# Retention plus switch MoE in one kernel: the order of rank, transpose and token steps around the first expert job, and the split of the last eviction

## The chip, the cores and the metric

The kernel runs on one core of a Trainium2 chip. The metric is the device time of one launch in microseconds (us), the median of several runs. All times below are microseconds unless marked ns; a time written like 98.18 is a moment, counted from the start of the profiled execution's span.

## What is computed

Inputs are q, k and v of shape (4, 8, 768, 64) in f32. The first stage is a retention (a linear attention whose state decays per head), the second a mixture of experts in which every token goes to one expert:

```python
gamma = 1.0 - 2.0 ** (-5.0 - np.arange(H))
for t in range(S):
    state = gamma * state + k[t] (outer) v[t]
    y[:, :, t] = q[t] @ state / sqrt(D)
x = y as (3072 tokens, 512)
logits = x @ w_gate + modality_bias[modality_id]
e = argmax(logits); gate = softmax(logits)[e]
out[token] = gate * (relu(x @ w1[e]) @ w2[e])      # w1: 512x1024, w2: 1024x512, 8 experts
```

## The kernel before

**Retention.** The 3072 tokens are 24 chunks of 128, six per batch entry. `two_chunks(n)` (L938) works on a pair of chunks at a time, and every engine gets its instructions in the order in which they are written there. For a pair n, n+1 the order on TensorE (PE) is: scores of the two chunks ahead (`scores`, L164, tile `sc`), the tokens of the two chunks behind (`tokens_out`, L216, tile `x`), the state part of the pair's heads (`heads_s`, L186, tile `y`), the masked part of chunk n (`heads_a`, L200, tile `y`), the state update of n+2 (`state`, L233, tile `st`), `heads_a(n+1)`, `state(n+3)`. VectorE (DVE) multiplies the scores by the mask into `abuf` (L176), scales the heads into `yT` (L214) and sums the gate logits `lg` (L229). ScalarE (ACT) scales q (`dq`, L153) and copies `x` out of PSUM into the token rows `xs` (L228) and the state `s` (L248). GpSimd (POOL) scales v (`vd`, L159).

**Buffers that tie the engines together.** All PSUM tiles come from one pool of eight banks, handed out in the order in which the readers of the earlier tiles are written; the state `st` holds one of them through a batch entry. The token rows `xs` have nine buffers (`XSB`, L44), so that the copy of chunk n waits until the rows of chunk n-9 have left.

**Routing.** After six chunks (a group; groups 0 to 3) the tokens get a place in the DRAM list `xsl`, ordered by expert: `route_a` (DVE; L315) makes the one-hot choice and the counts `cum`, `route_b` (PE, two small matmuls into `rk`; L353) the ranks, `route_c` (DVE; L360) the positions, `route_a` part 2 the gate's denominator (`den`, `rec`), and `scatter(g, i)` (POOL; L369) writes chunk i of the group to `xsl` with an indirect DMA (L378). Extra steps are hung into the pair loop with `at(n, place, ...)`, where the place is one of `top`, `st` (between the two scores), `sc` (after the second scores, or, in the pair's second half, between the two `heads_a`), `tk` (between the two `tokens_out`) and `end`.

**Jobs.** A job is 512 rows of one expert: 16 half stretches `first` (L714, tile `h_e` or `h_f`; six matmuls each, in three passes of split f32r numbers), then 16 `second` (L733, tile `o`). Weights are loaded with `raw` (L670, four buffers, issued on SyncE's queue), and split by `cut` (L675) into `hi` (ACT, L678) and `lo` (DVE, L683). The rows come with `rows_in` (L653, tile `xb`, SyncE's queue), are transposed by `flip_t` (DVE, L697) and split by `flip_hi` (ACT, L703) and `flip_lo` (DVE, L712). Two jobs (`e0`, `e1`) are chosen after group 1, at chunk 12, and the first starts when the last pair is done; group 3 is routed inside it: `last_tokens` (L1008) is a generator that goes on by one step after each stretch. Four further jobs (`f0` to `f3`) follow. The last job's last output tile is evicted from PSUM to `o` by DVE and ACT, half of the columns each (L750, L751), and then written by an indirect DMA (L754).

Of the kernel before, what the change touches and what calls it, by code (L numbers as in the profile page):

```python
# [11 lines left out]
AF = mybir.ActivationFunctionType  # L12
ALU = mybir.AluOpType
AX = mybir.AxisListType

P = 128
B, H, S, D = 4, 8, 768, 64
NT, DM, NE, DF = B * S, H * D, 8, 1024
NCH = S // P
NN = B * NCH  # L20
# [33 lines left out]
def kernel(  # L54
# [13 lines left out]
    nc = tc.nc  # L68
# [12 lines left out]
    def bank(name):  # L81
        return ps.tile([P, 512], F32, tag="bank", name=name)
# [133 lines left out]
    def tokens_out(n):  # L216
        yT, gr = yTs.pop(n), n // GRP
        if n % GRP == 0:
            lg[gr] = sm.tile([P, GRP, NE], F32, tag="lg", name=f"lg_{gr}")
        xs = xss[n] = wk.tile([P, NG, P + NE], F32, tag="xs", name=f"xs_{n}", bufs=XSB)  # L220
        for u in range(2):
            px = bank(f"x_{n}_{u}")[:, : 2 * (P + NE)].rearrange("p (g e) -> p g e", g=2)
            for g in range(2):
                nc.tensor.matmul(  # L224
                    px[:, g], yT[:, 2 * u + g], wgt[:, 2 * u + g], start=(g == 0), stop=(g == 1),
                    skip_group_check=True,
                )
            nc.scalar.copy(xs[:, 2 * u : 2 * u + 2], px)  # L228
        nc.vector.tensor_reduce(  # L229
            lg[gr][:, n % GRP], xs[:, :, P:].rearrange("p g e -> p e g"), axis=AX.X, op=ALU.add  # L230
        )
# [75 lines left out]
    def disjoint(ins, group):  # L307
        i = getattr(ins, "ins", ins)
        tc.declare_no_dep(i, group=group, reason="rows of different tokens")
        tc.add_to_no_dep_group(group, i)  # L310
# [42 lines left out]
    def route_b(gr):  # L353
        oh, ex = mid[gr]
        pr = bank(f"rk_{gr}")[:, : GRP * NE].rearrange("p (c e) -> p c e", e=NE)
        nc.tensor.matmul(pr, upper, oh, start=True, stop=False, skip_group_check=True)
        nc.tensor.matmul(pr, ones, cums[gr], start=False, stop=True, skip_group_check=True)
        mid[gr] = (oh, ex, pr)
# [59 lines left out]
    def ranks_a(t, counts):  # L418
        crep = sm.tile([P, NE, SPE], BF16, tag="crep", name=f"crep{t}")
        nc.vector.tensor_copy(crep, counts.unsqueeze(2).to_broadcast([P, NE, SPE]))  # L420
        mid["crep"] = crep.rearrange("p e i -> p (e i)")

    def ranks_p(t):
        crf = mid.pop("crep")
        pc = mid["pc"] = bank(f"pc{t}")
        nc.tensor.matmul(pc[:NCAND, :NCAND], ones[:, :NCAND], crf, start=True, stop=True)
        nc.tensor.matmul(pc[:NCAND, P : P + 1], crf, ones[:, 0:1], start=True, stop=True)
# [219 lines left out]
    def reg(lst, i, hi):  # L647
        return nc.values_load(lst[0:1, i : i + 1], engines=[SP], min_val=0, max_val=hi)

    def place(s, lst, i, j):  # L650
        s.row, s.e = reg(lst, i, EMPTY) * SLOT, reg(lst, j, NE - 1)
# [81 lines left out]
    def second(s, hh, part):  # L733
        if part == 0:
            s.po = bank(f"o{hh}_{s.tag}")
        for f in range(2 * part, 2 * part + 2):
            for k, (a, wi) in enumerate(PAIRS):
                nc.tensor.matmul(  # L738
                    s.po, s.hT[f][a][:, hh * P : (hh + 1) * P],
                    s.w[2][f // 2][wi][:, (f % 2) * DM : (f % 2 + 1) * DM],  # L740
                    start=(f == 0 and k == 0), stop=(f == FC - 1 and k == 2),
                )
        if part == 3:
            if hh == 0:
                s.o = me.tile([P, HH, DM], F32, tag="xb", name=f"o_{s.tag}")
            o = s.o[:, hh]
            gate = s.tg[:, hh, 1:2]
            if s is jobs[-1] and hh == HH - 1:
                h = DM // 2
                nc.vector.tensor_scalar(o[:, h:], s.po[:, h:], gate, None, op0=ALU.mult)  # L750
                nc.scalar.activation(o[:, :h], s.po[:, :h], AF.Copy, scale=gate)  # L751
            else:
                nc.scalar.activation(o, s.po, AF.Copy, scale=gate)  # L753
            ins = nc.gpsimd.indirect_dma_start(  # L754
                out=out[:, :],
                out_offset=bass.IndirectOffsetOnAxis(ap=s.tg.bitcast(I32)[:, hh, 0:1], axis=0),
                in_=o,
                in_offset=None,
                bounds_check=NT - 1,
                oob_is_err=False,  # L760
            )
            if s.tag != "dyn":
                disjoint(ins, "out_rows")
# [103 lines left out]
    def at(n, where, fn, *args):  # L867
        hooks.setdefault((n, where), []).append((fn, args))
# [12 lines left out]
    for g in range(NGRP - 1):  # L881
        t = (g + 1) * GRP
        at(t, "end", route_a, g, 0)
        at(t, "end", route_a, g, 1)
        at(t + 2, "st", route_b, g)
        early = g + 1 in EARLY
        if early:
            at(t + 2, "st", early_a, g + 1)
        at(t + 2, "st", route_c, g)
        at(t + 2, "st", route_a, g, 2)  # L890
        if early:
            a, b = EARLY[g + 1]
            at(t + 2, "st", early_b, g + 1)
            at(t + 2, "st", pick, a)
            at(t + 2, "end", place_early, a)
            at(t + 3, "end", mark, a)
            at(t + 3, "end", pick, b)
            at(t + 3, "end", mark, b)
            at(t + 3, "end", taken_a)
            at(t + 5, "end", taken_b)  # L900
            at(t + 4, "end", place_early, b)
        places = [(2, "end"), (3, "sc"), (4, "sc"), (4, "end"), (6, "sc"), (6, "end")]
        if early or t + 6 == NN:
            places[2:] = [(4, "sc"), (4, "end"), (5, "sc"), (5, "end")]
        for i, (k, where) in enumerate(places):
            at(t + k, where, scatter, g, i)

    t = GRP * min(EARLY)
    e = jobs[0]
    at(t + 2, "end", two, raw, e, 1, (0, 1))  # L910
    at(t + 3, "sc", two, raw, e, 1, (2, 3))
    at(t + 6, "top", rows_in, e)
    at(t + 6, "sc", cut, e, 1, 0, True)
    at(t + 6, "end", raw, e, 2, 0)
    n = t + 8
    at(n, "sc", flip_t, e, 0)
    at(n, "sc", flip_hi, e, 0)
    at(n, "tk", flip_lo, e, 0)
    at(n + 2, "top", flip_t, e, 1)
    at(n + 2, "top", flip_hi, e, 1)  # L920
    at(n + 2, "tk", flip_lo, e, 1)
# [85 lines left out]

    def last_tokens():  # L1008
        g = NGRP - 1
        tokens_out(NN - 1)  # L1010
        assert not hooks, hooks
        yield
        yield
        route_a(g, 0)
        yield
        yield
        route_a(g, 1)
        ranks_a("f", cnt[NGRP])
        yield
        yield  # L1020
        yield
        yield
        route_b(g)
        ranks_p("f")
        yield
        route_c(g)
        route_a(g, 2)
        yield
        scatter(g, 0)
        scatter(g, 1)  # L1030
        yield
        final_b()
        scatter(g, 2)
        scatter(g, 3)
        yield
        scatter(g, 4)
        scatter(g, 5)
        yield
        yield
        yield  # L1040
        final_c()
        yield
        final_d()
        for i in range(NLAST):
            place(jobs[NEARLY + i], lists["final"], i, U + i)
        for i, s in enumerate(rests):
            s.row = reg(lists["ends"], 1 + i, EMPTY) * SLOT
            s.e = reg(lists["final"], U + NLAST + i, NE - 1)
        yield
# [49 lines left out]
    with tc.manual_schedule(engines={PE, ACT, DVE, SP}):  # L1099
        load_kq(0, True)  # L1100
        nc.scalar.dma_start(cst, consts)
        nc.scalar.dma_start(gates, wgate)
        load_kv(0, True)
        load_kq(1)
        nc.sync.dma_start(dcq, decq)
        load_kv(1)
        for n in range(SINGLE, LEAD, 2):
            loads(n)
            if n == SINGLE + 2:
                setup_loads()  # L1110
        decay_v(0)
        at(0, "end", setup_a)
        at(1, "sc", setup_b)
        at(2, "sc", setup_rows)
        at(8, "end", setup_stores)
        at(5, "top", setup_c)
        at(7, "sc", list_consts)
        scores(0)
        for n in range(SINGLE):
            one_chunk(n)  # L1120
        first_pair(SINGLE)
        for n in range(SINGLE, NN, 2):
            two_chunks(n)
        tokens_out(NN - 2)
        r = last_tokens()
        for _ in all_jobs():
            next(r, None)
        assert next(r, "end") == "end"
# [4 lines left out]
    with tc.For_i(NLAST, nun, 1) as iv:  # L1133
        s = Job("dyn")
# [115 lines left out]
```

## Time and profile before

| | us |
|---|---|
| median of 3 runs | 391.22 |
| lowest and highest run | 389.74, 391.63 |
| the profiled execution | 389.86 |
| its span, first to last instruction | 388.0 |
| PE busy in the span | 371.4 |

The profile gives the busy time of each engine, a timeline (start, duration, engine, line, operation, output<-inputs, shapes, count of merged instructions, and in brackets the idle time of the engine just before, with what ended it), and tables of waits. PE means TensorE matmuls. Instructions of the same kind that follow each other on one engine are merged into one row, so a row's duration can hold gaps.

### The profile page before, as it was taken

The page shows a single profiled execution, that of the slowest core. Times are in us where ns is not written, and L with a number is a line of the kernel's source. Part 1 is how long each engine was busy: PE and PEld are TensorE (multiplying, and loading weights), DVE is VectorE, ACT ScalarE, POOL GpSimd, SP SyncE. Part 2 cuts the span into 40 slices and gives each one's busy share as a digit, 9 for nine tenths or more (in the row PEclk, how much of TensorE's full clock was granted, in tenths as well). Part 3 has the DMA queues.
Part 4 walks back from the last instruction along what each step waited for, and adds up shares of the span by engine and source line. Part 5 has one row for each costly group of instructions (what it writes and reads, how often), then busy time and mean ns, then how long its engine had stood idle before and what let it go on. Part 6 is the DMA issues. An engine that isn't in the chain of part 4 may idle for free.

```text
span 388.0 us, 7932 instructions
## 1 busy us (share of the span) xinstructions
PE 371.4 (96%) x2963; PEld 312.2 (80%) x2963; DVE 203.0 (52%) x417; ACT 156.6 (40%) x303; POOL 99.7 (26%) x141
## 2 busy tenths in 40 slices
PE   3999999999799999999999999999999999999993
PEld 3999898898688788888887888778888888888882
DVE  1676867778578982348343282433823466144100
ACT  1355536454566352435433354234532345234110
POOL 1342375574710787100220102101021002100121
PEclk9999999999999999999999999999999999999998
DMA  7999799999439758587972969729342584400001
GB/s 268 398 377 398 299 312 359 349 406 212 182 102 238 221 227 303 200 173 244 329 313 66 213 215 328 300 82 193 110 162 110 148 176 135 164 28 3 27 27 52
DMA packets 40330, 81.94 MB, mean 211 GB/s; under 512 B 8029, under 2 KB 20445, under 8 KB 40033
## 3 DMA queue, kind: packets, MB, share of 16 engines
q1 hardware_dynamic: 34720, 65.72, 53.8%
q0 software_dynamic: 5136, 15.21, 10.0%
q8 instruction: 25, 0.41, 0.5%
q10 hardware_dynamic: 432, 0.46, 0.4%
q14 instruction: 17, 0.14, 0.1%
HBM read 65.05 MB, written 23.41 MB: 228 GB/s over the span
## 4 chain that ended last, share of the span: by engine, by line
issue 56%; PE 23%; POOL 9%; DVE 4%; DMA 4%; POOLq 1%; ACT 1%; ACTq 0%
POOL out_dram L754 5%; PE sc L171 5%; PE x L224 5%; PE y L207 4%; PE h_e L720 4%; PE y L195 2%; PE st L243 2%; DMA out_dram<-o_e,tg_e 2%; DMA cst<-in_consts_dram 1%; POOL xsl L378 1%; POOL xsl L628 1%; DMA raw_e<-in_w_dram 1%; DVE cum L342 1%; POOL vd L159 1%; POOL out_dram L850 1%
## 5 line engine op out<-in xcount | busy, mean ns | idle before, releaser
L720 PE MATMUL h_f<-xT_f,hi_f 128*128 128x512 f32 x256 | 81.1, 392 | 0.0
L738 PE MATMUL o_f<-hi_f,hT_f 128*128 128x512 f32 x256 | 78.8, 389 | 0.0
L683 DVE TENSOR_TENSOR lo_f<-raw_f,hi_f 128x1024 fp32r<-128x1024 f32 x32 | 39.2, 1225 | 34.4 <-ACT hi_f L678 34.1
L720 PEld LDWEIGHTS h_f<-xT_f,hi_f 128*128 128x128 f32 x256 | 48.1, 188 | 11.1 <-issue 1.2
L738 PEld LDWEIGHTS o_f<-hi_f,hT_f 128*128 128x128 f32 x256 | 48.0, 188 | 10.0
L728 DVE SCALAR_TENSOR_TENSOR hT_f<-h_f,hT_f 128x512 fp32r<-128x512 f32 x32 | 22.1, 692 | 63.2 <-ACT hT_f L727 63.2
L720 PE MATMUL h_f<-xT_f,lo_f 128*128 128x512 f32 x128 | 49.9, 390 | 0.0
L738 PE MATMUL o_f<-lo_f,hT_f 128*128 128x512 f32 x128 | 49.8, 389 | 0.0
L754 POOL DMA_INDIRECT out_dram<-o_f,tg_f x16 | 15.7, 983 | 127.1 <-ACT o_f L753 116.8
L727 ACT ACTIVATE hT_f<-h_f 128x512 fp32r<-128x512 f32 x32 | 19.1, 597 | 54.5 <-PE h_f L720 54.5
L720 PE MATMUL h_e<-xT_e,hi_e 128*128 128x512 f32 x128 | 40.6, 393 | 0.0
L738 PE MATMUL o_e<-hi_e,hT_e 128*128 128x512 f32 x128 | 39.5, 390 | 0.0
L176 DVE TENSOR_TENSOR abuf<-sc,cst 128x512 f32<-128x512 f32 x48 | 30.1, 680 | 16.7 <-PE sc L171 16.7
L171 PE MATMUL sc<-kq 64*128 64x128 f32 x384 | 28.8, 294 | 5.6 <-DMA kq<-in_qkv_dram 5.1
L159 POOL TENSOR_TENSOR vd<-kv,cst 128x512 f32<-128x512 f32 x24 | 24.9, 1044 | 33.5 <-PE y L207 14.4
L678 ACT CAST hi_f<-raw_f 128x1024 fp32r<-128x1024 f32 x32 | 33.3, 1041 | 0.0
L171 PEld LDWEIGHTS sc<-kq 64*128 64x128 f32 x384 | 25.2, 199 | 8.2 <-DMA kq<-in_qkv_dram 5.1
L738 PEld LDWEIGHTS o_f<-lo_f,hT_f 128*128 128x128 f32 x128 | 24.0, 188 | 5.0
L720 PEld LDWEIGHTS h_e<-xT_e,hi_e 128*128 128x128 f32 x128 | 24.0, 188 | 4.9
L738 PEld LDWEIGHTS o_e<-hi_e,hT_e 128*128 128x128 f32 x128 | 23.9, 188 | 4.9
L720 PEld LDWEIGHTS h_f<-xT_f,lo_f 128*128 128x128 f32 x128 | 24.0, 188 | 4.8
L753 ACT ACTIVATE o_f<-o_f,tg_f 128x512 f32<-128x512 f32 x15 | 10.3, 689 | 42.9 <-PE o_f L738 42.9
(165 smaller groups left out, 521.7 us busy)
## 6 DMA issues: line engine op xcount, KB each, us to landing
raw_f<-in_w_dram SPq DMA_DIRECT2D x32, 512.0 KB, 3.5
kq<-in_qkv_dram SPq DMA_DIRECT2D x23, 512.0 KB, 9.2
kv<-in_qkv_dram SPq DMA_DIRECT2D x19, 512.0 KB, 9.9
raw_e<-in_w_dram SPq DMA_DIRECT2D x16, 512.0 KB, 5.6
xb_f<-xsl SPq DMA_DIRECT2D x16, 256.0 KB, 5.4
abuf<-in_w_dram SPq DMA_DIRECT2D x8, 512.0 KB, 6.2
rw<-in_w_dram SPq DMA_DIRECT2D x16, 256.0 KB, 7.1
xb_e<-xsl SPq DMA_DIRECT2D x8, 256.0 KB, 5.3
```

Of the source, the lines that this page charges most:

```text
L159: nc.gpsimd.tensor_tensor(vds[n], vv, dec[:, n % NCH].unsqueeze(2).to_broadcast([P, H, D]), op=ALU.mult)
L171: nc.tensor.matmul(pe[j][:, g * P : (g + 1) * P], kt[r, g], qt[r, g], start=True, stop=True, skip_group_check=True,)
L176: nc.vector.tensor_tensor(a[:, j], pe[j].rearrange("p (h t) -> p h t", t=P), mask.unsqueeze(1).to_broadcast([P, NG, P]), op=ALU.mult,)
L207: nc.tensor.matmul(py[j][g % 2 * D : (g % 2 + 1) * D, g // 2], vd[:, 2 * g + j], a[:, j, g], start=(first and g < 2), stop=(g >= 2), skip_ ...
L224: nc.tensor.matmul(px[:, g], yT[:, 2 * u + g], wgt[:, 2 * u + g], start=(g == 0), stop=(g == 1), skip_group_check=True,)
L678: nc.scalar.copy(hi, t)
L683: nc.vector.tensor_tensor(lo, t, hi.bitcast(F32), op=ALU.subtract)
L720: nc.tensor.matmul(s.ph, s.w[1][f // 2][wi][:, o : o + P], s.xT[kc][a], start=(kc == 0 and k == 0), stop=(kc == KC - 1 and k == 2),)
L727: nc.scalar.activation(hi, s.ph, AF.Relu)
L728: nc.vector.scalar_tensor_tensor(lo, s.ph, 0.0, hi.bitcast(F32), op0=ALU.max, op1=ALU.subtract)
L738: nc.tensor.matmul(s.po, s.hT[f][a][:, hh * P : (hh + 1) * P], s.w[2][f // 2][wi][:, (f % 2) * DM : (f % 2 + 1) * DM], start=(f == 0 and k ...
L754: ins = nc.gpsimd.indirect_dma_start(out=out[:, :], out_offset=bass.IndirectOffsetOnAxis(ap=s.tg.bitcast(I32)[:, hh, 0:1], axis=0), in_=o, ...
```

## The change

Four edits. In groups 0 and 2 the rank matmuls (`route_b`) go from between the pair's two scores to between the pair's two `tokens_out`, and `route_c` and the denominator from there to after both; the group's first two scatters go one place later each. The first job's first transpose and its split go from before the tokens of the pair 20, 21 to after them. The loads of the first job's third and fourth piece of w1 go behind `rows_in` on SyncE's queue. The tokens of chunk 22 go from before the first job to after its first stretch, and those of chunk 23 to after its second. The last eviction is halved by partitions (0 to 63 DVE, 64 to 127 ACT) in place of columns, and the two halves are declared independent.

```diff
             if s is jobs[-1] and hh == HH - 1:
-                h = DM // 2
-                nc.vector.tensor_scalar(o[:, h:], s.po[:, h:], gate, None, op0=ALU.mult)
-                nc.scalar.activation(o[:, :h], s.po[:, :h], AF.Copy, scale=gate)
+
+                a, b = slice(0, D), slice(D, P)
+                ins = nc.vector.tensor_scalar(o[a], s.po[a], gate[a], None, op0=ALU.mult)
+                disjoint(ins, "halves")
+                ins = nc.scalar.activation(o[b], s.po[b], AF.Copy, scale=gate[b])
+                disjoint(ins, "halves")
...
         at(t, "end", route_a, g, 1)
-        at(t + 2, "st", route_b, g)
         early = g + 1 in EARLY
+        at(t + 2, "st" if early else "tk", route_b, g)
         if early:
             at(t + 2, "st", early_a, g + 1)
-        at(t + 2, "st", route_c, g)
-        at(t + 2, "st", route_a, g, 2)
+        at(t + 2, "st" if early else "end", route_c, g)
+        at(t + 2, "st" if early else "end", route_a, g, 2)
...
-        places = [(2, "end"), (3, "sc"), (4, "sc"), (4, "end"), (6, "sc"), (6, "end")]
-        if early or t + 6 == NN:
-            places[2:] = [(4, "sc"), (4, "end"), (5, "sc"), (5, "end")]
+        places = [(3, "sc"), (3, "end"), (4, "sc"), (4, "end"), (6, "sc"), (6, "end")]
+        if t + 6 == NN:
+            places[4:] = [(5, "sc"), (5, "end")]
+        if early:
+            places = [(2, "end"), (3, "sc"), (4, "sc"), (4, "end"), (5, "sc"), (5, "end")]
...
     at(t + 2, "end", two, raw, e, 1, (0, 1))
-    at(t + 3, "sc", two, raw, e, 1, (2, 3))
     at(t + 6, "top", rows_in, e)
+    at(t + 6, "top", two, raw, e, 1, (2, 3))
...
     n = t + 8
-    at(n, "sc", flip_t, e, 0)
-    at(n, "sc", flip_hi, e, 0)
-    at(n, "tk", flip_lo, e, 0)
+    at(n + 1, "top", flip_t, e, 0)
+    at(n + 1, "top", flip_hi, e, 0)
+    at(n + 1, "sc", flip_lo, e, 0)
...
     def last_tokens():
         g = NGRP - 1
+        tokens_out(NN - 2)
+        yield
         tokens_out(NN - 1)
         assert not hooks, hooks
-        yield
         yield
         route_a(g, 0)
...
-        tokens_out(NN - 2)
         r = last_tokens()
```

## Rows read from the trace of the kernel before

**Rows 1.** The page: busy time, share of the span and instructions of each engine
```profile
PE 371.4 (96%) x2963; PEld 312.2 (80%) x2963; DVE 203.0 (52%) x417; ACT 156.6 (40%) x303; POOL 99.7 (26%) x141
```
**Rows 2.** Waits of PE: line, what it waited for, us in total, times, longest
```profile
PE y L195 <- ACT xs L228: 2.1, 1, 2.1
PE x L224 <- DVE yT L214: 0.6, 1, 0.6
PE rk L357 <- DVE cum L343: 0.4, 1, 0.4
```
**Rows 3.** Timeline, chunks 20 to 23: start, us, engine, line, what [idle before]
```profile
92.71 0.75 DVE L214 TENSOR_TENSOR yT<-y,dcq 128x256 f32<-128x256 f32 x2
...
93.18 1.49 PE L171 MATMUL sc<-kq 64*128 64x128 f32 x16 [0.15 <-DVE yT L214]
...
...
94.60 2.12 PE L224 MATMUL x<-wgt,yT 128*128 128x136 f32 x16
95.23 0.20 DVE L363 TENSOR_TENSOR rkt<-rk,oh 128x48 f32<-128x48 f32 x1
...
95.89 0.19 DVE L350 RECIPROCAL rec<-den 128x6 f32<-128x6 f32 x1
96.00 1.25 DVE L176 TENSOR_TENSOR abuf<-sc,cst 128x512 f32<-128x512 f32 x2
...
96.65 1.08 PE L195 MATMUL y<-kq,s 64*64 64x128 f32 x18
96.95 1.04 POOL L378 DMA_INDIRECT xsl<-xs,pos  x1 [0.54 <-POOL xs L374]
...
98.18 0.71 DVE L697 STREAM_TRANSPOSE x_e<-xb_e 128x512 f32<-128x512 f32 x1 [0.93 <-DMA xb_e<-xsl]
...
98.92 0.62 ACT L703 CAST xT_e<-x_e 128x512 fp32r<-128x512 f32 x1 [6.09 <-DVE x_e L697]
99.44 1.24 ACT L228 COPY xs<-x 128x272 f32<-128x272 f32 x4
...
99.88 0.66 PE L195 MATMUL y<-kq,s 64*64 64x128 f32 x14 [2.15 <-ACT xs L228]
...
105.92 1.97 PE L207 MATMUL y<-abuf,vd 128*64 128x128 f32 x32
...
107.97 0.75 DVE L214 TENSOR_TENSOR yT<-y,dq 128x256 f32<-128x256 f32 x2
108.53 1.16 PE L224 MATMUL x<-wgt,yT 128*128 128x136 f32 x8 [0.65 <-DVE yT L214]
```
**Rows 4.** Chain of work around the first job's start: start, us, engine and line
```profile
109.70 1.39 PE h_e L720 x6
```
**Rows 5.** Timeline, group 0's first scatter, and what ran 8 us later
```profile
47.30 1.18 POOL L378 DMA_INDIRECT xsl<-xs,pos  x1 [0.76 <-ACT xs L228]
...
55.33 0.68 ACT L228 COPY xs<-x 128x272 f32<-128x272 f32 x2 [1.58 <-PE y L195]
...
56.87 0.37 ACT L248 COPY s<-st 128x256 f32<-128x256 f32 x1 [0.87 <-PE st L243]
...
57.47 0.63 PE L243 MATMUL st<-vd,kv 128*64 128x64 f32 x16
```
**Rows 6.** Landing of scatters after issue: group 0's first; all 24 (shortest: group 2)
```profile
DMA to landing us min/median/max: 7.9/7.9/7.9
...
DMA to landing us min/median/max: 2.8/6.7/9.4
```
**Rows 7.** Timeline, the end of the last job
```profile
376.23 0.69 ACT L753 ACTIVATE o_f<-o_f,tg_f 128x512 f32<-128x512 f32 x1 [4.75 <-PE o_f L738]
...
381.67 0.48 DVE L750 TENSOR_SCALAR o_f<-o_f,tg_f 128x256 f32<-128x256 f32 x1 [20.38 <-PE o_f L738]
382.19 0.47 ACT L751 ACTIVATE o_f<-o_f,tg_f 128x256 f32<-128x256 f32 x1 [5.27 <-DVE o_f L750]
382.93 0.98 POOL L754 DMA_INDIRECT out_dram<-o_f,tg_f  x1 [4.76 <-ACTq L1133]
```

## The prediction
> **What bounds the kernel now.** I read the page first: PE is busy for 371.4 of 388.0 us [rows 1], so a change pays only where PE stands still or where the end comes after PE's last matmul. Then PE's table of waits, which is short: behind the wait for the first inputs, which the change does not touch, the longest is 2.1 us for ACT's copies of `x`, then 0.6 us for `yT` and 0.4 us for the rank's counts [rows 2]. Then the timeline around them [rows 3]. It shows one chain: DVE's first transpose waits for the rows of job e0 until 98.18, ACT's split of it (98.92) waits 6.09 us for the transpose, ACT's copies of `x`, which are written behind that split, start only at 99.44, and PE, which needs a bank that those copies free, stands from 97.73 to 99.88 in the middle of the state part of chunk 21. Last, the timelines of group 0's first scatter [rows 5] and of the end [rows 7].
>
> **Part 1, the last pairs and the first job.** What is removed is the order in which ACT's copies stand behind a DMA. I walk PE's path with the rows' durations.
> The second scores of the pair begin at 93.18 and take 1.49 us, where 16 such matmuls without a wait take about 1.0 (32 of the masked part: 1.97); they wait for the first `yT` [rows 3]. Without the rank in front they take a bank one earlier in the ring: the stall ends when half of the `yT` row is done, 92.71 + 0.38 = 93.1, and the scores at 94.1, not 94.6. `x` 18 (1.03, half of the pair's 2.06 from 94.60 to 96.66), two rank matmuls (0.15, my estimate from the two waiting pieces of [rows 2] being gone) and `x` 19 (1.03) end at 96.3. The heads of chunk 20 now need both masks of the second scores; DVE's masks take 0.64 each [rows 3] and follow one another from 94.1, so they end at 96.65. So PE is at the heads of chunk 20 at 96.7, as before: this half microsecond is given back.
> From here there is a gain. The copies of `x` 18 need only `x` 18, so the heads of chunk 21 go on at once and end at 97.7 (two times 0.5 us), where they ended at 99.88 + 0.66 = 100.54: **2.8 us earlier**. PE's path from there to the end of the masked part of chunk 23 was 107.89 - 100.54 = 7.35 us without a wait [rows 3], so it would end at 105.05. DVE decides whether it can: gate sums 0.4, rank 0.85 (95.23 to 96.08), so 98.0; transpose when the rows are there, 98.2 to 98.9; `yT` 20 to 99.6; low half 0.7 (the transpose's row, same shape) to 100.3; `yT` 21 to 101.05. PE needs `yT` 20 at 99.95 and 21 at 101.0: no wait. The next transpose (101.75), its split on ACT (102.4) and the copies of `x` 20 (0.4 each) free the last bank at 102.8; PE wants it at 102.65. I charge 0.2: PE ends at 105.25.
> Then the wait for `yT` 22. Behind the copies (103.2) DVE has a gate sum, a low half, a transpose, a gate sum, a transpose and a low half: 0.2 + 0.7 + 0.7 + 0.2 + 0.7 + 0.7 = 3.2, so `yT` 22 runs from 106.4 to 107.15 (107.97 before). The job's first half stretch now stands in front of `x` 22: 105.25 + 1.39 [rows 4] = 106.65, and half a `yT` is there at 106.8. The 0.65 us wait becomes 0.1. In sum 107.89 - 105.25 = 2.64, plus 0.65 - 0.1: **3.2 us gained**. The margin at `yT` 22 is nothing, so what delays DVE or ACT in these 8 us costs as much.
>
> **Part 2, group 0.** The same exchange, with no DMA behind it, so PE's share is about 0.1 us gained. But the rank's results now come behind both masks and both gate sums, about 1.6 us later than before (two masks 1.25, two sums 0.4), and with them the group's first scatter: from 47.30 to 48.9. The first copy of chunk 9 uses the buffer of chunk 0; it ran at 55.33 after 1.58 us of idle time, and the scatter landed 7.9 us after its issue, at 55.2 [rows 5, 6]; the engine that the row names had long been done. So ACT waits for that landing. Behind it stand the copies (0.68) and the state's copy (0.37), and PE's next state update cannot begin before that copy has read the bank. It began at 57.47; it can begin 1.25 us after a landing. With the same 7.9 us the landing is at 56.8 and the update at 58.05: **0.6 us lost**. The ends: a landing of 2.8 us loses nothing, one of 9.4 us, the longest [rows 6], loses 2.1. I take 7.9, for the same stretch has the same loads in flight.
>
> **Part 3, the end.** ACT's half waited for DVE's: DVE 381.67 to 382.15, ACT 382.19 to 382.66, and the DMA 0.27 later [rows 7]. Side by side, ACT needs 0.69 for 512 columns [rows 7] and DVE 0.48 + 0.25 = 0.73 (256 further columns cost 0.26: a mask of 512 takes 0.64, half a `yT` row of 256 0.38 [rows 3]). The DMA starts at 381.67 + 0.73 + 0.27 = 382.67: **0.26 us gained**. If they still went one after the other, 0.73 + 0.04 + 0.69 would lose 0.47.
> What the row shows is an order by semaphore, not its cause. The Trainium skill (PSUM — Partial Sum Buffer, section PSUM bank collisions raise a hardware error) says that two engines may not touch the same bank in the same group of 32 partitions at once, disjoint columns included, and may in different groups. By it column halves had to wait and partition halves need not; by the reading that a bank takes one engine at a time they would still wait. The trace agrees as far as the first half goes.
>
> **Part 4, the loads.** Two pieces of w1 go behind `rows_in`. The first of them is wanted by the job's ninth half stretch, 8 times 1.39 us behind its start at 105, and `rows_in` has landed by 98.2, so the work of the last pairs and 8 half stretches hide them and they cost nothing; without that cover a piece would hold PE for its landing, 2.8 to 9.4 us by the nearest rows [rows 6]. On SyncE's queue nothing else is moved past but one piece of w2. In front of the rows there is 1 MB less in flight, so the last scatter and the rows land no later; the transpose at 98.2 above takes no gain from it. Moving the tokens of 22 and 23 into the job moves no DMA.
>
> **Sum.** 3.2 + 0.1 - 0.6 + 0.26 = 3.0 us. The profiled execution took 389.86 (span 388.0 and 1.86 around it) and would take 386.9; the median of the runs is 391.22, 1.36 above that execution, so I forecast 391.22 - 3.0 = **388.2**.
>
> **The rivals.**
> *A better case:* the scatter of group 0 lands within 7.2 us and costs nothing: 3.6 us, 387.6. For it speaks that group 2's scatters land in as little as 2.8 us, against it that this one took 7.9 [rows 6].
> *The wait comes back on the row buffers.* The copies of `x` 21 need the buffer of chunk 12, the first scatter of group 2. It was issued at 96.95 [rows 3]; the rank now ends 1.9 us later, so 98.9. ACT wants the buffer at 103.2: 4.3 us. The shortest landings, 2.8, are this group's, but now two pieces of w1 and one of w2 may be in flight beside it. At the median landing, 6.7 us [rows 6], ACT, the transposes behind it and `yT` 22 come 2.4 later: gain 0.6, 390.6. The Trainium skill (DMA: Bandwidth & Descriptors, section Queues, rings and completion order) says that a DMA engine takes turns between the queues that have work for it, so weight loads would stretch a scatter; the two ends of [rows 6] agree.
> *Slower:* the same place, with a landing of 9.4 us: 108.3, so 5.1 later, 3.0 - 5.1 = 2.1 slower, 393.3. It turns into a loss from a landing of 7.3 us on. It needs the load of the retention's middle in a stretch without chunk loads.
> *The halves still run in turn* (the change would not do what it says): 0.73 less gain, 388.9.
> *DVE becomes the bound:* the rows land 1 to 2 us later than 98.2, or the low halves are held up; `yT` 20 or 22 slips by as much and the gain is 1.5: 389.7.
>
> **How the numbers follow.** Forecast 0.55, better 0.10, wait back 0.15, slower 0.05, in turn 0.08, DVE bound 0.07. A measurement of this kernel tells about 0.5% from no change, 1.96 us. Below 389.26 are the forecast (all but 0.05 of it, for the runs spread over 1.9 us), the better case and most of the halves in turn: 0.67. Within 0.5%: 0.28; slower 0.05. The range goes from 386.2 (the better case less the runs' spread) to 390.8 (the wait come back); the forecast's own is 387.2 to 389.4.
>
> **What would show it.** Right: no wait of PE for `xs` near 98, ACT's `xs` copies in front of the first `xT_e` cast, no wait for `yT` at the job's start, the last ACT and DVE halves starting together. Wrong: ACT idle before the `xs` copies of chunk 21 or longer than 3 us before those of chunk 9, PE waiting at `st` near 58, ACT's last half behind DVE's. The forecast falls if PE's idle time before the job is not at least 2.5 us less.

## The result and the profile after

| | before | after |
|---|---|---|
| median, us | 391.43 (10 runs) | 388.05 (10 runs) |
| lowest and highest run | 389.74, 392.54 | 386.49, 390.08 |
| the profiled execution | 389.86 | 386.49 |
| its span | 388.0 | 384.6 |

The ratio of after to before is 0.992, with a 95% interval of 0.989 to 0.994: 3.2 us less (2.2 to 4.1). The forecast was 3.0 us less.

Single executions of one kernel differ by more than the gain (those of the changed kernel run from 386.49 to 390.08), and both profiled executions lie 1.6 us under the median of their kernel. So a part of the change that is worth half a microsecond must be read from its own stretch. The table cuts the spans at PE instructions that every kernel has (the first score matmul of a chunk, the first matmul of job e0's fifth half stretch `h_e`, PE's last matmul, the start of the last output DMA); each number is a difference of two start times in the trace of one execution.

| stretch, us | before | after | flip_only | ranks_only | tokens_only | best | noranks | noranks_again |
|---|---|---|---|---|---|---|---|---|
| start to scores of chunk 6 | 25.97 | 25.03 | 25.24 | 25.31 | 25.88 | 25.82 | 25.21 | 26.43 |
| to scores of chunk 10 | 15.36 | 15.36 | 15.36 | 15.36 | 15.36 | 15.36 | 15.36 | 15.36 |
| to scores of chunk 14 (group 0's ranks) | 16.70 | 17.62 | 16.71 | 17.49 | 16.71 | 16.55 | 16.71 | 16.71 |
| to scores of chunk 18 | 17.24 | 16.89 | 16.93 | 16.76 | 17.00 | 16.78 | 16.90 | 16.68 |
| to scores of chunk 22 | 15.83 | 16.90 | 16.89 | 16.98 | 17.09 | 18.08 | 18.58 | 17.65 |
| to the fifth half stretch (job start) | 24.87 | 20.57 | 23.30 | 25.96 | 23.76 | 20.61 | 22.09 | 23.09 |
| to PE's end | 265.65 | 265.65 | 265.65 | 265.65 | 265.65 | 265.65 | 265.65 | 265.65 |
| PE's end to the last DMA | 1.31 | 1.55 | 1.31 | 1.30 | 1.31 | 1.00 | 1.00 | 1.00 |
| to the end of the span | 5.05 | 5.05 | 5.05 | 5.06 | 5.05 | 5.49 | 5.05 | 5.07 |

Three stretches answer to the three parts of the sum: the job start gained 4.30, group 0 lost 0.92, the end lost 0.24, together 3.14 gained. The other stretches differ as well, by amounts that the parts do not explain: the start alone takes 24.81 to 26.55 us in the fourteen profiles. The stretch to the scores of chunk 22 is odd: 15.83 in the profile of before, 16.88 to 18.58 in all thirteen others, though flip_only, ranks_only and tokens_only change nothing in it. So that profile of before came about 1.1 us early to the last pairs, and part of its 24.87 may be a longer wait for the rows: taken together, the two stretches from the scores of chunk 18 to the job's fifth half stretch went from 40.70 to 37.47, which is 3.23 us less. There is one profile of before, so the profiles leave the gain at the job start between 3.2 and 4.3. The timed runs speak for the upper half: 3.2 us (2.2 to 4.1) is what is left after the two losses of 0.92 and 0.24.

PE's waits in the profile after (line, what it waited for, us in total, times, longest):

```profile
PE sc L171 <- DMA kq<-in_qkv_dram: 5.3, 1, 5.3
PE st L243 <- POOL vd L159: 1.8, 3, 0.8
PE y L207 <- issue: 0.6, 2, 0.3
PE sc L171 <- DVE yT L214: 0.3, 1, 0.3
```

The three rows of [rows 2] have left this table. The wait for `vd` has grown: before had it once, with 0.8 us, in a row that [rows 2] does not show. PE's busy time on the page fell from 371.4 to 369.5 us with the same 2963 matmuls, so some standstill had been counted as busy.

The timeline of the last pair and the job's start in the profile after (columns as in [rows 3]):

```profile
94.35 1.19 PE L224 MATMUL x<-wgt,yT 128*128 128x136 f32 x8
95.17 0.81 ACT L228 COPY xs<-x 128x272 f32<-128x272 f32 x2 [1.64 <-issue]
95.38 0.19 PE L356 MATMUL rk<-oh,upper 128*128 128x48 bf16 x1
...
96.54 1.10 PE L195 MATMUL y<-kq,s 64*64 64x128 f32 x32
...
97.84 0.19 DVE L350 RECIPROCAL rec<-den 128x6 f32<-128x6 f32 x1
98.14 0.71 DVE L697 STREAM_TRANSPOSE x_e<-xb_e 128x512 f32<-128x512 f32 x1
...
98.91 1.04 POOL L378 DMA_INDIRECT xsl<-xs,pos  x1 [0.55 <-POOL xs L374]
98.96 1.05 PE L207 MATMUL y<-abuf,vd 128*64 128x128 f32 x16
...
99.94 2.12 PE L224 MATMUL x<-wgt,yT 128*128 128x136 f32 x16
...
105.67 0.75 DVE L214 TENSOR_TENSOR yT<-y,dq 128x256 f32<-128x256 f32 x2
...
106.43 1.09 PE L224 MATMUL x<-wgt,yT 128*128 128x136 f32 x8
```

ACT's copies now start at 95.17, three microseconds ahead of the transpose. That the transpose starts at 98.14, as good as the 98.18 of before [rows 3], is chance: there it waited for the rows, here it follows DVE's rank work (`rec` ends at 98.03) and waits for nothing. All 32 matmuls of the heads are one row without a hole (96.54 to 97.64), where [rows 3] has two rows with 2.15 us between them. `x` of chunk 22 starts at 106.43 with no bracket.

### The profile page after: what moved, and what is told of

It reads as the page before. It is cut to its first block, busy times and chain, and to the rows that moved or that the text cites. A ratio compares the mean times of both kernels' runs of the same rounds, so it can differ in the third digit from the quotient of the medians.

```text
span 384.6 us, 7930 instructions
## 1 busy us (share of the span) xinstructions
PE 369.5 (96%) x2963; PEld 310.2 (81%) x2963; DVE 202.5 (53%) x417; ACT 157.1 (41%) x303; POOL 100.8 (26%) x141
## 4 chain that ended last, share of the span: by engine, by line
PE 86%; DVE 4%; DMA 3%; issue 2%; POOL 2%; ACT 1%; POOLq 0%
PE h_f L720 23%; PE o_f L738 22%; PE h_e L720 11%; PE o_e L738 11%; PE x L224 5%; PE sc L171 4%; PE y L207 3%; PE y L195 2%; PE st L243 2%; DMA kv<-in_qkv_dram 1%; DMA kq<-in_qkv_dram 1%; POOL vd L159 1%; DVE cum L342 1%; PE ro L844 1%; PE rh L822 1%
## 5 line engine op out<-in xcount | busy, mean ns | idle before, releaser
L171 PE MATMUL sc<-kq 64*128 64x128 f32 x384 | 27.7, 288 | 5.8 <-DMA kq<-in_qkv_dram 5.3
L171 PEld LDWEIGHTS sc<-kq 64*128 64x128 f32 x384 | 24.3, 193 | 7.7 <-DMA kq<-in_qkv_dram 5.3
```

What stands on the lines that cost most here:

```text
L171: nc.tensor.matmul(pe[j][:, g * P : (g + 1) * P], kt[r, g], qt[r, g], start=True, stop=True, skip_group_check=True,)
```

## The experiments

All of them are read against the table above and the ratio to the kernel before.

**One part alone: the first transpose.**

```diff
-    at(n, "sc", flip_t, e, 0)
-    at(n, "sc", flip_hi, e, 0)
-    at(n, "tk", flip_lo, e, 0)
+    at(n + 1, "top", flip_t, e, 0)
+    at(n + 1, "top", flip_hi, e, 0)
+    at(n + 1, "sc", flip_lo, e, 0)
```

> The kernel before with one edit: the first job's first transpose and its split go behind the tokens of the pair 20, 21. Measure: the stretch from PE's start of the scores of chunk 22 to the start of the job's third half stretch, 22.3 us before and 18.0 after the whole change. My theory: this edit alone takes out the 2.15 us in which PE waited for ACT's copies, but the wait for yT 22 at the job's start grows from 0.65 to about 1.2, since DVE's chain is shortened by less than PE's: stretch 20.3 us, total about 2.0 us faster. Rival: the rank's place is what holds the pair, and the transpose only fills idle time: stretch within 0.6 us of 22.3, total the same.

Measured: 389.92 us, ratio 0.996 (0.994 to 0.998), or 1.7 us less. The wait for `xs` is gone and the wait for `yT` at the job's start has grown, as expected:

```profile
PE x L224 <- DVE yT L214: 1.2, 1, 1.2
PE sc L171 <- DVE yT L214: 0.2, 1, 0.2
```

The job start gained 1.57 us, 0.4 less than expected (the expectation counts to an earlier half stretch of the job, so its figures are some 2.6 us smaller). What may have eaten the rest stands in its timeline in the masked part of chunk 21 (L207): two matmuls at 98.68, then nothing until 99.31.

```profile
97.95 1.01 POOL L378 DMA_INDIRECT xsl<-xs,pos  x1 [0.28 <-POOL xs L374]
98.05 0.72 PE L243 MATMUL st<-vd,kv 128*64 128x64 f32 x15
...
98.68 0.33 PE L207 MATMUL y<-abuf,vd 128*64 128x128 f32 x2
...
99.31 1.19 PE L207 MATMUL y<-abuf,vd 128*64 128x128 f32 x13 [0.29 <-issue]
```

**One part alone: the ranks of groups 0 and 2.**

```diff
-        at(t + 2, "st", route_b, g)
+        at(t + 2, "st" if early else "tk", route_b, g)
...
-        at(t + 2, "st", route_c, g)
-        at(t + 2, "st", route_a, g, 2)
+        at(t + 2, "st" if early else "end", route_c, g)
+        at(t + 2, "st" if early else "end", route_a, g, 2)
```

(with the scatters' places as in the change)

> The kernel before with one edit: rank matmuls between the pair's two token steps, and the group's first two scatters one place later, in groups 0 and 2. My theory: PE still stands for ACT's copies in the pair 20, 21, so the half microsecond at the scores is given back there: the stretch from the scores of chunk 22 to the third half stretch stays at 22 us; and in group 0 the first scatter is issued 1.6 us later, lands later, and ACT and the state update behind it wait: the stretch from the scores of chunk 10 to those of chunk 14 grows from 16.7 to 17.6. Total 0.5 to 1 us slower. Rival: the rank exchange is a gain of its own, 0.5 us at each of the two groups: total 1 us faster, stretch at group 0 16.2.

Measured: 392.44 us, ratio 1.002 (0.999 to 1.005), which can't be told from no change. In its profile group 0 lost 0.79, as expected, and the job start, which was to stay as it was, lost 1.09:

```profile
98.15 0.71 DVE L697 STREAM_TRANSPOSE x_e<-xb_e 128x512 f32<-128x512 f32 x1 [1.47 <-DMA xb_e<-xsl]
...
99.85 1.30 PE L195 MATMUL y<-kq,s 64*64 64x128 f32 x16 [2.46 <-ACT xs L228]
...
101.54 0.19 DVE L350 RECIPROCAL rec<-den 128x6 f32<-128x6 f32 x1
```

The old chain is still there, with a longer wait for the rows in this execution (1.47 us in front of the transpose, 0.93 before), and DVE's rank work now hangs on its end: `rec` at 101.54, where before had 95.89 [rows 3].

**One part alone: the tokens of chunks 22 and 23.**

```diff
     def last_tokens():
+        tokens_out(NN - 2)
+        yield
         tokens_out(NN - 1)
...
-        tokens_out(NN - 2)
         r = last_tokens()
```

> The kernel before with one part done alone: the tokens of chunk 22 behind the job's first half stretch, those of chunk 23 behind the second. Theory: only PE's wait of 0.65 us for yT at the job's start goes; the wait of 2.1 us for the copies of x stays; the stretch from the scores of chunk 22 to the fifth half stretch goes from 24.9 to about 24.2 us, and the time by at most 0.6 us. Rival (the two x tiles inside the job keep their banks longer and hold the h tiles up): the 0.65 us come back as a wait at the second or third half stretch, and nothing is gained.

Measured: 390.82 us, ratio 0.999 (0.997 to 1.001). PE's waits:

```profile
PE y L195 <- ACT xs L228: 1.2, 1, 1.2
...
PE x L224 <- DVE yT L214: 0.3, 1, 0.3
```

The wait at the job's start is gone (the 0.3 us are `x` of chunk 21). The job start is 1.11 us shorter, but 0.9 of that is the shorter wait for `xs`, in an execution whose rows were there earlier: its transpose began 5.71 us after the scores of chunk 22, that of before 7.07. So the tokens' move is worth a few tenths, and the time can't tell it from nothing.

**The change without the transpose's move.**

```diff
-    at(n + 1, "top", flip_t, e, 0)
-    at(n + 1, "top", flip_hi, e, 0)
-    at(n + 1, "sc", flip_lo, e, 0)
+    at(n, "sc", flip_t, e, 0)
+    at(n, "sc", flip_hi, e, 0)
+    at(n, "tk", flip_lo, e, 0)
```

> The changed kernel with one part undone: the first job's first transpose and its split stand in front of the tokens of chunks 20 and 21 again. Theory (the gain sits in this move): the copies of x for chunks 18 and 19 wait for the transpose again, PE stands 2 us or more in the heads of chunk 21, and the stretch from the scores of chunk 22 to the job's fifth half stretch is 23.0 to 24.5 us, where the changed kernel has 20.6 and the kernel before 24.9; about 3 us slower than the changed kernel, within 0.3% of the kernel before. Rival (the exchange of the ranks and the tokens' move into the job carry the gain): the stretch stays under 21.5 us.

Measured: 391.87 us (388.3 to 393.45), ratio 1.002 (0.999 to 1.004): with this part undone the whole gain is gone, as the theory said. The size of the stretch was missed, 22.44 instead of 23.0 to 24.5. The profiled execution is the shortest of the ten, and its rows were early, the transpose at 5.05 us after the scores of chunk 22:

```profile
96.88 0.71 DVE L697 STREAM_TRANSPOSE x_e<-xb_e 128x512 f32<-128x512 f32 x1 [0.25 <-issue]
...
98.15 1.24 ACT L228 COPY xs<-x 128x272 f32<-128x272 f32 x4
...
98.58 0.95 PE L195 MATMUL y<-kq,s 64*64 64x128 f32 x16 [1.24 <-ACT xs L228]
```

Even so PE waits 1.24 us for the copies behind the transpose's split.

**The change without the loads' move.**

```diff
+    at(t + 3, "sc", two, raw, e, 1, (2, 3))
     at(t + 6, "top", rows_in, e)
-    at(t + 6, "top", two, raw, e, 1, (2, 3))
```

> The changed kernel with one part undone: the third and fourth piece of w1 in front of the first job's rows on SyncE's queue again. Theory: the load of the rows starts 1 to 1.5 us later than 87.9, as in the kernel before (89.2), the last scatter and the rows land up to 0.5 us later, the first transpose starts at 98.2 to 98.6 where it started at 98.14, and the heads of chunk 23 are held up by no more than that: within 0.5 us of the changed kernel. Rival (the loads' move carries part of the gain): the transpose starts after 99, and the stretch from the scores of chunk 22 to the fifth half stretch is over 21.6 us instead of 20.6.

Measured: 387.91 us, ratio 0.9925 (0.990 to 0.995), the same as with the change; the job start took 20.45. The load of the rows (SP's row) did not come later but 4.92 us ahead of the scores of chunk 22 (93.42), where after has 3.87, so this detail of the expectation was wrong; the transpose waited for nothing:

```profile
88.50 2.03 SPq L660 DMA_DIRECT2D xb_e<-xsl  x4
...
99.64 0.71 DVE L697 STREAM_TRANSPOSE x_e<-xb_e 128x512 f32<-128x512 f32 x1
```

**Group 0's ranks back in their old places,** the rest as in the change (for group 0 alone `route_b`, `route_c` and `den` at `st` again, and the scatters' old places).

> The changed kernel with the ranks and scatters of group 0 as they were (group 2 as changed). My theory: the first scatter is issued about 1.6 us earlier against PE's path, lands before ACT needs the row buffer of chunk 9, and the state update of chunk 13 no longer waits: scores of chunk 10 to scores of chunk 14 16.7 us in place of 17.6, total 0.9 us faster than the change. Rival: the longer stretch comes from a disturbance that wanders from run to run and not from the scatter: 17.6 or any value between, with no change of the idle time in front of the copies of chunk 9 (4.0 us).

Measured: 387.34 us, ratio 0.988 (0.984 to 0.992); the stretch took 16.81 us, and ACT's idle time in front of the copies of chunk 9 is down to 1.16 us. The theory holds.

**The last tile by ACT alone,** the rest as in the change.

```diff
-            if s is jobs[-1] and hh == HH - 1:
...
-            else:
-                nc.scalar.activation(o, s.po, AF.Copy, scale=gate)
+            nc.scalar.activation(o, s.po, AF.Copy, scale=gate)
```

> The changed kernel, but ACT alone evicts the last output tile, as all others. My theory: with the two halves the output DMA waits for two engines; POOL takes one of the two waits as an instruction of its own in front, and only behind it prepares the DMA, which then starts 0.77 us after the last half; with one engine to wait for it starts 0.27 us after. So from the end of PE's last matmul to the DMA's start 0.69 + 0.27 = 0.96 us, where the change has 1.55 and the kernel before 1.30: total 0.6 us faster than the change. Rival: the 0.77 us belong to the half tiles themselves (64 partitions), or vary from run to run, and one engine's 512 columns cost as much as two halves: within 0.1 us of the change.

Measured: 387.62 us, ratio 0.988 (0.984 to 0.992); PE's end to the DMA 1.00 us.

```profile
380.29 0.69 ACT L748 ACTIVATE o_f<-o_f,tg_f 128x512 f32<-128x512 f32 x1 [4.75 <-PE o_f L738]
381.25 0.98 POOL L749 DMA_INDIRECT out_dram<-o_f,tg_f  x1 [4.45 <-ACTq L1130]
```

**The last tile by DVE alone,** to see whether the engine matters or the number of waits.

> The changed kernel, but its last output tile is evicted by DVE alone (512 columns, 128 partitions). Theory (the output's DMA waits for two engines, and one of the two waits stands in front of the DMA as an instruction of its own, so that the DMA starts late): with one engine to wait for, the DMA starts about 0.27 us after DVE's end, so PE's end to the DMA is 0.04 + 0.74 + 0.27 = 1.05 us, against 1.55 with the two halves. Rival (a signal from DVE takes longer to release GpSimd's DMA than one from ACT): about 0.77 us after DVE's end, so 1.55 again.

Measured (one execution, 386.13 us): the DMA starts 0.28 us after DVE's end (377.93 + 0.75 = 378.68), 1.07 after PE's. So it is not DVE as such, and the number of waits is left. The first fence is the timeline; the second is POOL's queue in the same kernel (line, operation, count, shortest, median and longest duration in ns, start): the instruction in front of the DMA took 17 ns.

```profile
377.93 0.75 DVE L749 TENSOR_SCALAR o_f<-o_f,tg_f 128x512 f32<-128x512 f32 x1 [20.37 <-PE o_f L738]
378.96 0.98 POOL L752 DMA_INDIRECT out_dram<-o_f,tg_f  x1 [4.52 <-DVEq L1133]
```
```profile
L752 POOLq EVENT_SEMAPHORE  x1: 17/17/17, 373.3 to 373.3; - x1
```

**Both losses taken out** (group 0's ranks as before, the last tile by ACT alone), beside the change itself and a kernel that has group 2's ranks in their old places too, on one chip.

> The changed kernel with the two parts that cost time taken out: group 0's ranks and scatters in their old places, and the last tile evicted by ACT alone. Theory (both costs are real and add up): 0.8 to 0.9 us from group 0 (stretch from the scores of chunk 10 to those of chunk 14 at 16.7 to 16.8 instead of 17.6) and 0.55 us from the end (PE's end to the DMA 1.00 instead of 1.55): 1.4 us faster than the changed kernel on the same chip, a ratio to the kernel before of about 0.988. Rival (what is gained at group 0 is given back before the first job, because the job's rows arrive when the loads let them and not when PE does): only the 0.55 us of the end remain.

> The changed kernel once more, beside the other two on one chip: the ratio to the kernel before is 0.992 again, 3.0 to 3.4 us.

> As the kernel with the two costly parts taken out, and with group 2's ranks and scatters in their old places too: what is left of the change is the move of the first transpose, of the tokens of chunks 22 and 23, and of the two loads. Theory by the prediction's walk (the half microsecond that the ranks' move saves in front of the scores comes back as a wait for the masks, but DVE then has its rank work off the critical stretch of its queue): the stretch from the scores of chunk 22 to the fifth half stretch is 20.6 to 21.2 us, so no more than 0.6 us slower than with the ranks moved. Rival (the ranks between the two x are what gives DVE room): as with the first transpose moved alone, PE waits for yT of chunk 20 for 1 us or more, the stretch is over 22 us, and the kernel is 1.5 us or more slower.

Measured: best 387.05 us, ratio 0.990 (0.988 to 0.992); the change 388.42, ratio 0.993 (0.991 to 0.995); noranks 389.00, ratio 0.996 (0.993 to 0.999). The two costs add up as expected: 1.37 us between best and the change (each ratio is known to about 0.2%, 0.8 us), expected 1.4. On this chip best is faster than before and after; whether it beats the kernels with one cost taken out (0.988 each, 0.984 to 0.992, on another chip) the runs don't tell. For noranks the rival was right about the time, and the theory wrong: 1.95 us slower than best. But the rival's reason, a wait for `yT` of chunk 20, is not in its profile. There the masked part of chunk 21 took 1.93 us instead of 1.0, as in flip_only. Whether that lay there by chance was asked next.

> The kernel with only the moves of the first transpose, of the tokens and of the loads, a second time. In its first profile the stretch from the scores of chunk 22 to the fifth half stretch took 22.09 us, and the masked part of chunk 21 in it 1.93 us where about 1.0 is usual. Theory (that standstill wanders and lies there by chance): the masked part of chunk 21 takes about 1.0 us now and the stretch 20.9 to 21.4. Rival (it belongs to this order of the ranks and scatters): the masked part of chunk 21 takes over 1.7 us again, and the stretch 22 or more.

Measured: 389.37 us, ratio 0.996 (0.993 to 0.998). The standstill came again: the masked part of chunk 21 took 1.60 us, a little under the 1.7 that the rival asked for and far from the 1.0 of the theory, and the stretch 23.09.

```profile
99.54 1.01 POOL L378 DMA_INDIRECT xsl<-xs,pos  x1 [0.28 <-POOL xs L374]
99.65 0.64 PE L243 MATMUL st<-vd,kv 128*64 128x64 f32 x16
100.16 0.53 PE L207 MATMUL y<-abuf,vd 128*64 128x128 f32 x5
...
100.88 0.88 PE L207 MATMUL y<-abuf,vd 128*64 128x128 f32 x11 [0.19 <-issue]
100.92 0.76 DVE L214 TENSOR_TENSOR yT<-y,dq 128x256 f32<-128x256 f32 x2 [1.76 <-PE st L243]
...
103.88 1.32 PE L224 MATMUL x<-wgt,yT 128*128 128x136 f32 x7 [1.00 <-DVE yT L214]
```

The same place in best, where group 2's ranks, and with them its scatters, come later:

```profile
99.33 0.64 PE L243 MATMUL st<-vd,kv 128*64 128x64 f32 x16
99.61 0.72 DVE L214 TENSOR_TENSOR yT<-y,dq 128x256 f32<-128x256 f32 x2
...
99.74 1.04 POOL L378 DMA_INDIRECT xsl<-xs,pos  x1 [0.55 <-POOL xs L374]
99.79 1.05 PE L207 MATMUL y<-abuf,vd 128*64 128x128 f32 x16
```

In noranks_again POOL is issuing a scatter while PE does the state update; PE stops five matmuls into the masked part and goes on 0.33 us after the scatter's issue ends (100.55). In best the scatter begins with the masked part, and nothing stops. The stop is not all of the difference: it is 0.9 us of noranks' 1.5 in this stretch and 0.6 of the 2.5 here. Here PE also waits 1.00 us for `yT` of chunk 21 (103.88), a wait of the kind that the rival named, one chunk later.

## Why the prediction was right, and where not

**The sum** was right, 3.0 forecast and 3.2 (2.2 to 4.1) measured, but partly by luck, because errors cancel: in the profiles the job start gained 4.30 where 3.2 was forecast, group 0 lost 0.92 where 0.5 was, and the end lost 0.24 where 0.26 was to be gained.

**Part 1, the walk.** The mechanism is right: PE's wait for `xs` is gone, and undoing the transpose's move (flip_back) takes the whole gain away. The moments hold closely on the clock. Heads of chunk 21 done: 97.7 forecast, 97.64 measured. End of the last masked part: 105.25 against 104.99. `x` of chunk 22: 106.65 to 106.8 against 106.43, without a wait, where the forecast left 0.1. But this closeness is luck in part, since this execution began the scores of chunk 22 at 91.81, 0.70 later than the profile from which the walk set out (91.11). Counted from those scores, the heads of chunk 20 begin after 4.73 us, where before took 5.54 and the walk left that as it was; 0.81 is gained there. From the heads of chunk 20 to the fifth half stretch PE took 15.84 us instead of 19.33, 3.49 less, and the seven profiles with both the transpose and group 2's ranks moved all have 15.83 to 15.89.

The step that failed is the share of the ranks. The walk found that their half microsecond "is given back" and credited them nothing at the job's start; it looked only at PE's banks and DVE's masks. In front of the heads of chunk 20 they save 0.81 against the profile of before, but only 0.1 to 0.4 against the four others with group 2's ranks in the old place and no such early start (4.82 to 5.09). Behind it they matter more: with the transpose moved they are worth 1.5 to 2.5 in the whole stretch (20.61 in best, 22.09 and 23.09 without them; 1.95 us by the medians). They set when POOL issues group 2's scatters, and without their move PE stops beside one of these issues. That stop is 0.9 and 0.6 us of it; how the rest comes about, the wait for `yT` of chunk 21 in noranks_again included, stays open. The parts do not add: transpose, tokens and ranks alone change the stretch by -1.57, -1.11 and +1.09, together -1.6, and the change as a whole by -4.30. The ratios of the timed runs say the same: 1.7 and 0.3 us faster, and 0.8 slower with group 0's 0.79 in it, so about 2 us together.

**The rival of the row buffers** (group 2's first scatter, issued at 98.9, holds up ACT's copies of `x` 21) was walked to the right moment, 98.91, but ACT did not wait: its copies ran from 102.25 in one row of four. **DVE as the bound** did not come either: the transpose at 98.14 did not wait for the rows.

**Part 2, group 0.** Forecast 0.6 lost less 0.1 gained; measured 0.92 lost, and 0.79 with the ranks alone. The fact is right, its size about half. In the profile after, the waits that were foretold stand in these rows:

```profile
54.84 1.01 POOL L378 DMA_INDIRECT xsl<-xs,pos  x1 [0.28 <-POOL xs L374]
...
55.20 0.70 PE L207 MATMUL y<-abuf,vd 128*64 128x128 f32 x8
...
56.20 0.68 PE L207 MATMUL y<-abuf,vd 128*64 128x128 f32 x8 [0.30 <-issue]
...
56.35 0.67 ACT L228 COPY xs<-x 128x272 f32<-128x272 f32 x2 [4.01 <-PE y L207]
...
56.91 0.39 ACT L248 COPY s<-st 128x256 f32<-128x256 f32 x1
...
57.40 0.69 PE L243 MATMUL st<-vd,kv 128*64 128x64 f32 x16 [0.53 <-POOL vd L159]
```

ACT's 4.01 us of idle time are the wait that was foretold ("longer than 3 us before those of chunk 9"), although the row names PE. With PE's wait at `st` near 58 it was listed as a sign of being wrong; both came, and both belong to this part, not to the sum. The trace keeps semaphore updates of the landing of the group's first scatter: the last is at 56.25, 8.31 us after the issue at 47.94, and ACT's copies start 0.10 us after it, in before too (55.23 and 55.33). PE's state update at 57.40 starts 0.10 us after ACT's copy of the state ends (56.91 + 0.39), although its row names POOL; that is 1.15 us after the landing, where the forecast had 1.25. Both distances of 0.10 us stand in all seven executions with group 0's ranks moved. So the loss goes the way that the prediction described, and the term that it had too small is the landing: it took 7.9 for granted, and the seven took 8.3 to 8.6. ([rows 6] itself rests on 15 of the 24 scatters, those whose landing the profile gives.) The 0.1 us that PE was to gain does not show, since PE waits for the landing anyway.

PE also stopped by itself: at 55.90, in the middle of the masked part of chunk 11, to go on at 56.20, 0.34 after the end of a scatter's issue at 55.85. This was in no step. All seven executions show it at the same place, and in group0_back and best it is gone with the long wait; but PE was done with that masked part at 56.88 and waited for ACT until 57.40, so the stop itself cost nothing here. Whether the same issue also made the landing late, no run here tells.

**Part 3, the end,** was wrong in sign: 0.26 gained was forecast, 0.24 lost measured. Its first step was right:

```profile
378.07 0.68 ACT L753 ACTIVATE o_f<-o_f,tg_f 64x512 f32<-64x512 f32 x1 [4.75 <-PE o_f L738]
378.07 0.74 DVE L751 TENSOR_SCALAR o_f<-o_f,tg_f 64x512 f32<-64x512 f32 x1 [20.38 <-PE o_f L738]
379.58 0.99 POOL L757 DMA_INDIRECT out_dram<-o_f,tg_f  x1 [5.01 <-DVEq L1138]
```
```profile
L757 POOLq EVENT_SEMAPHORE  x1: 5417/5417/5417, 373.4 to 373.4; - x1
```

The halves start in the same moment, at 378.07, and take 0.68 and 0.74 as costed. This trace agrees with the Trainium skill (PSUM — Partial Sum Buffer, section PSUM bank collisions raise a hardware error): different groups of partitions of one bank can be read side by side. What column halves would do without the wait for each other, no run here shows.

The step that failed is "the DMA 0.27 later". That number held in before because there the DMA had only ACT to wait for: ACT's half itself waited for DVE's, and the instruction in front of the DMA on POOL's queue does not wait for DVE (by the semaphores that the trace lists) and took 17 ns:

```profile
L754 POOLq EVENT_SEMAPHORE  x1: 17/17/17, 377.0 to 377.0; - x1
```

With the halves independent, the DMA has to wait for both engines, and the wait for DVE stands on POOL in that instruction in front of the DMA: it lasted 5.417 us, from 373.44 to 378.85, and the DMA came 0.73 after it, 0.77 after DVE. All five profiles with the two halves have this 0.77. The kernels that wait for one engine have 0.27 (ACT) and 0.28 (DVE).

**Part 4, the loads,** at nothing: right (0.9925 without the move, 0.9919 with it).

## What to carry to other kernels

When ACT's or DVE's queue holds work that waits for a DMA, move everything else in front of it. Here nothing was gained without that move, and yet alone it brought 1.7 us and its full worth only with the ranks moved too; so undo the parts of a change one at a time as well as doing them one at a time. A moved step takes its DMA issues along: ask what the other engines do in the microsecond in which GpSimd issues them. An instruction with two late waits is no longer the one whose start delay was measured with one, so an eviction split over two engines can cost more at its DMA than it saves. And moments that match the forecast on the clock prove little if the stretch began at another moment: compare the distances.

## What the runs showed of the hardware

**PE can stop beside a scatter's issue.** Take, in the fourteen profiled executions, the masked part of each chunk from 7 on and in it the longest distance between the starts of two matmuls (0.10 to 0.15 us as a rule). It is over 0.2 us thirty times, up to 0.64, and in 28 of the thirty PE goes on 0.32 to 0.38 us after the end of a scatter's issue on POOL. Of 32 scatters whose issue began at least 0.3 us ahead of the masked part of an odd chunk, beside the state update, and ended after its first matmul, 27 came with such a stop; the other five show that it need not come, and the group was picked out in the same traces that it is counted in. PE's records name no releaser ("issue"). DVE and ACT can be held up with it: in noranks_again DVE starts `yT` of chunk 20 only at 100.92, after 1.76 us of idle time and 0.37 after the end of the same issue. What it is that stops PE stays open: no run here changed the scatter itself.

**A DMA with two late waits starts late.** It started 0.77 us after the later engine, in five executions, against 0.27 and 0.28 with one engine to wait for.
